# A linear-attention and channel-mix kernel with a written-out order: pairs in couples, one-piece q exponentials, single-DMA stores, a new order

## The chip, the cores and the metric

The kernel runs on one core of a Trainium2 chip. The metric is the device time of one launch in microseconds (us), the median over runs. Matrix products run on TensorE (PE), vector work on VectorE (DVE), exponentials and other activations on ScalarE (ACT), further elementwise work on GpSimd (POOL). SyncE (SP), POOL and ACT issue DMAs.

## The reference

There are 8 batches of 8 heads, 576 positions and 64 channels per head. Cut to what matters:

```
def phi(x):                                   # x: q or k
    proj = x @ w_phi                          # 64 -> 128 features
    proj = proj - max(abs(proj), axis=-1)
    return concat([exp(proj), exp(-proj)])    # 256 features
kv  = phi(k).T @ v ;  z = sum(phi(k))         # per head
att = (phi(q) @ kv) / (phi(q) @ z + 1e-6)     # 576 x 64 per head
x      = att, heads side by side              # 576 x 512 per batch
x_prev = x shifted by one position
xk = mu_k*x + (1-mu_k)*x_prev ;  xr likewise with mu_r
k  = relu(xk @ w_k)                           # 512 -> 1024
v  = (k*k) @ w_v                              # 1024 -> 512
out = sigmoid(xr @ w_r) * v
```

(As published, the reference subtracts the maximum before the minus sign is applied, so exp(-proj) carries the maximum with the opposite sign; the kernel does the same.)

## The kernel before

The heads are taken two at a time: pair n = 4b + a is pair a of batch b, 32 pairs in all. Each partition holds nine neighbouring positions of one head, 64 partitions a head. k and q of a pair lie side by side as nine blocks of 128 columns, two positions each; the middle block holds k's last position and q's first, and is handled as an "edge", for all four pairs of a batch at once (in three parts for batch 0). The second part works batch by batch on 8 blocks of 64 positions, in output tiles of 128 rows (`ci` 0 to 3); the ninth blocks of two batches form an edge tile, made once per two batches.

Everything is an operation with a name, given to `op()` and issued in the order of the text `ORDER`, written out in full. In it a word is a name, `:i` the PSUM buffer it writes, `/ENG` the engine that runs it, and `+n@i` says that n fill products on ones (L295) stand before it on PE. Every engine runs its own operations in that order. The names used here, with the pair number or batch.part behind them:

- `lk`, `lq`, `lv`: loads of k, q and v. `pt`, `pa`, `pb`: transposes on PE and copies for batches 0 and 1; later batches are transposed by DMA (`tr`).
- `kp`, `qp` (L561): projections, 8 products with 64 rows each. `rk`, `rq` (L574, L579): negated maxima of absolute values, 128x8, on DVE.
- `ea`, `eb` (L600): exponentials of k, plus and minus, 128x1024 on ACT. `em` (L586): exponentials of k's maxima, which `va`, `vb` (L592) multiply into v, mostly on POOL.
- `mh` (L610, L611): q's maxima split into two bf16 parts; `mt` (L615): their transpose on PE; `mc`: the copy out of PSUM; `qt` (L625, L631): q's projection with features on partitions, plus the maxima by products with the selector `sel`.
- `qa`, `qb` (L639): exponentials of q, each in two halves of 512. `kv` (L652, L658) and its copy `kc`; `nd` (L673): numerator and denominator; `ra`, `rd` (L681, L685): the division.
- `xz` (DMA transpose on SP) or `xt`, `xe`, `xf` (for the first 8 pairs, on PE): the result with channels on partitions; `xu`: the shifted copy; `df`, `xa`, `xb` (L722, L728): difference, xk and xr.
- `h`, `rl`, `sq`: product with w_k, relu, square, eight column blocks a batch; `r`, `th`: product with w_r, tanh; `v` (L836), `ob` (L842): product with w_v, output step; `so` (L849): two stores of 64 rows each. `he`, `rle`, `sqe`, `re`, `the`, `ve` (L920), `obe` (L924), `soe` (L929): the same for edge tiles.

`kp`, `qp`, `qt`, `kv` and the edge's `tp` and `qte` use products with 64 rows of the array, two side by side; all others use 128 rows. Large PSUM tiles have three buffers, one-bank tiles two. `h`, `r` and the edge products ask for all `xb` of the batch, and `xb` for `xa`.

Of the kernel before, what the change touches and what calls it, by code (L numbers as in the profile page):

```python
# [8 lines left out]
FP = mybir.dt.float32  # L9
# [10 lines left out]
ones hk hq ident dve2 hk.d hq.d wphi wphi.d lk0.1 lk0.1.d lq0.1 lq0.1.d lv0.0/SP lv0.0.d lk0.2  # L20
lk0.2.d dve3 mus mus.d lq0.2 lq0.2.d lv0.1/POOL lv0.1.d lk0.0.d/DVE lk1.0 lk1.0.d lv0.2/SP lv0.2.d
lq0.0.d/DVE pt0.0:0+9@0 lq1.0 lq1.0.d pt0.1:1 pa0/DVE pb0/ACT tr0 lk1.2 lk1.2.d dve1 tp0.0:0+1@2
kp0:1 rt0.0 qp0:2 lq1.2 lq1.2.d rk0 ekt0.0 pt1.0:1+1@0 eme0.0 pt1.1:0 wk.0 wk.0.d pa1/ACT pb1/DVE
tr1 mhe0.0/POOL rq0 ea0 kp1:0+2@2 eb0 rk1 qp1:2+2@0 mh0/POOL wk.1 wk.1.d wk.d mt0:1 em0 tp0.1:1
mte0.0:0 ea1 mce0.0/DVE va0/POOL mc0/DVE rt0.1 pt2.0:0 pt2.1:1 pa2/DVE ekt0.1 vb0/POOL pb2/DVE tr2
eb1 qt0:1 rq1 pt3.0:1 eme0.1 lv1.0/POOL lv1.0.d pt3.1:0 qa0 qp2:0 pa3/DVE kv0:2 mh1/POOL pb3/DVE tr3
rq2 wr.0 wr.0.d qte0.0:1 kc0/ACT em1 tp0.2:2 mhe0.1/POOL qb0 mt1:0 rt0.2 kp2:0 va1/POOL rk2 mc1/ACT
ekt0.2 qp3:1 eqe0.0 vb1/POOL kp3:2+1@0 rq3 ea2 mte0.1:0 mhe0.2/POOL pt4.0:1+2@1 eb2 mce0.1/DVE kv1:1
pa4/DVE mh2/POOL rk3 qte0.1:0 eme0.2 pt4.1:1 mh3/POOL nd0:0 eqe0.1 wr.1 wr.1.d wr.d em2 mt2:0
kc1/DVE mc2/ACT pb4/DVE tr4 wv.0 wv.0.d ea3 qt1:1 ra0 rd0 pt5.0:1 va2/POOL eb3 pt5.1:0 pa5/DVE qp4:0  # L30
pb5/DVE tr5 wv.1 wv.1.d wv.d mte0.2:1 qa1 rq4 qp5:2 pt6.0:0 vb2/POOL qb1 mce0.2/DVE pa6/DVE qte0.2:1
qt2:0 lk2.0 lk2.0.d rq5 em3 eqe0.2 xt0:0 va3/POOL kp4:1 qa2 xf0/DVE xe0/DVE kv2:2 rk4 mh4/POOL mt3:0
pt6.1:1 kc2/ACT df0/POOL qb2 nd1:2 mc3/DVE pb6/DVE tr6 mt4:0 ea4 ra1 nd2:0 mc4/DVE lq2.0 lq2.0.d rd1
pt7.0:0 eb4 lv1.2/POOL lv1.2.d ra2 xt1:1 rd2 kp5:2 vb3/POOL xf1/ACT xe1/ACT qt3:1 rk5 pa7/ACT
pt7.1:1 mh5/POOL kv3:0 qa3 xa0 xt2:0 xb0 qb3 pb7/DVE tr7 xf2/ACT df1/DVE xe2/ACT tp1.0:1 kc3/DVE ea5
rt1.0 df2/POOL nd3:0+1@1 eb5 ra3 mhe1.0/POOL rd3 ekt1.0 qt4:2+4@1 xa1 xt3:0 eme1.0 mt5:1 xb1 mc5/ACT
xe3/ACT qt5:1+1@2 xa2 qa4 mte1.0:1 qp6:0 xb2 xf3/ACT qb4 df3/DVE mce1.0/DVE xa3 em5 qte1.0:1+2@0 em4
kp6:2 xb3 eqe1.0 va4/POOL rq6 r0.0:0+3@0 qa5 h0.0:1 vb4/DVE qb5 rk6 mh6/POOL kv4:0 tr2.0 tr2.0.d tr8
tr9 rl0.0/ACT vb5/POOL qp7:1 th0.0 h0.1:1 rq7 ea6 va5/POOL r0.1:0 kc4/DVE em6 rl0.1/ACT sq0.0/DVE
tr2.2 tr2.2.d tr10 tr11 kv5:0 vb6/DVE th0.1 kp7:1 eb6 mh7/DVE mt6:1 h0.2:0 rk7 sq0.1/POOL nd4:2  # L40
lk3.0 lk3.0.d mc6/DVE em7 rl0.2/DVE h0.3:1 kc5/ACT lv2.0/SP lv2.0.d vb7/POOL ea7 ra4 rd4 lv2.2/SP
lv2.2.d h0.4:0 eb7 rl0.3/DVE va7/POOL qp8:2 xt4:1 rl0.4/ACT rq8 nd5:1 va6/POOL sq0.3/ACT qt6:0
sq0.2/ACT xf4/DVE xe4/DVE tp2.0:2 lq3.0 lq3.0.d ra5 qa6 h0.5:0 rd5 sq0.4/POOL qb6 rt2.0 h0.6:1 lk4.0
lk4.0.d rl0.5/ACT kv6:1 rl0.6/DVE df4/POOL ekt2.0 qp9:0 kc6/DVE h0.7:0 rq9 sq0.5/ACT mhe2.0/POOL
mt7:1 kp8:2 rl0.7/ACT kv7:1 mc7/DVE mh8/POOL rk8 sq0.7/ACT kp9:0 sq0.6/POOL mte2.0:0 r0.2:1 eme2.0
kc7/ACT em8 xa4 nd6:1 mce2.0/ACT th0.2 xb4 v0.0:0 ea8 rk9 vb8/POOL eb8 v0.1:1 va8/POOL em9 ob0.0 ea9
ra6 so0.0 so0.0.d rd6 mh9/POOL eb9 lq4.0 lq4.0.d qte2.0:0 ob0.1 qp10:1 vb9/POOL eqe2.0 qt7:2 rq10
qp11:0 tr3.0 tr3.0.d tr12 tr13 r0.3:1 qa7 va9/POOL rq11 xt5:0 th0.3 kp10:1 mh10/POOL qb7 xe5/DVE
xt6:1 xf5/DVE rk10 kv8:0 df5/POOL tr3.2 tr3.2.d tr14 tr15 xe6/ACT mt8:0 nd7:2 kc8/ACT xf6/DVE
mc8/DVE ea10 mt9:1 xa5 qt8:0 v0.2:0 eb10 df6/DVE mc9/DVE ra7 xa6 em10 qa8 xb5 qt9:1 xb6 qb8 v0.3:1  # L50
ob0.2 va10/POOL qa9 rd7 vb10/POOL mt10:0 nd8:0 qb9 mc10/DVE ob0.3 xt7:0 ra8 kv9:2 mh11/POOL xf7/ACT
rd8 xe7/ACT kv10:1 kc9/ACT df7/DVE xz8 xz8.d qt10:0 kc10/ACT xa7 kp11:2 qa10 nd9:1 xb7 mt11:0 qb10
rk11 r1.0:1 mc11/ACT nd10:0 ra9 th1.0 rd9 r1.1:0 em11 ea11 ra10 vb11/POOL xz9 xz9.d rd10 kp12:1
th1.1 h1.0:1 rk12 va11/POOL eb11 so0.1 so0.1.d qp12:0 h1.1:0 rq12 ea12 xu8/POOL xz10 xz10.d df8/POOL
qt11:2 rl1.1/ACT rl1.0/DVE tp3.0:0 eb12 lv3.0/SP lv3.0.d h1.2:0 rt3.0 sq1.0/POOL so0.2 so0.2.d qa11
kp13:1 rl1.2/DVE mh12/POOL h1.3:1 tr4.0 tr4.0.d tr16 tr17 qb11 sq1.1/DVE sq1.2/POOL h1.4:0 rl1.3/DVE
ekt3.0 xa8 r1.2:1 eme3.0 sq1.3/DVE rl1.4/ACT qp13:0 rk13 mhe3.0/POOL kv11:2 tr4.2 tr4.2.d tr18 tr19
th1.2 em12 xu10/POOL mt12:0 h1.5:1 sq1.4/ACT xu9/POOL mc12/DVE va12/POOL kc11/DVE ea13 rq13 h1.6:0
vb12/POOL rl1.5/ACT nd11:2 rl1.6/DVE lv3.2/SP lv3.2.d em13 sq1.5/ACT qp14:0 xb8 mte3.0:1 h1.7:0 eb13
mh13/POOL mce3.0/DVE ra11 he0.0:1 rd11 sq1.6/POOL rl1.7/ACT rq14 sq1.7/ACT xz11 xz11.d mt13:0 lk5.0  # L60
lk5.0.d kv12:2 rle0.0/ACT qt12:1 mc13/ACT df9/DVE kc12/ACT kp14:0 df10/DVE qa12 qte3.0:0 qt13:2 xa9
v1.0:1 eqe3.0 xa10 rk14 mh14/POOL qb12 vb13/POOL v1.1:0 ea14 xb9 eb14 va13/POOL ob1.0 nd12:1 ob1.1
em14 mt14:1 tp4.0:0 mc14/ACT ra12 qa13 vb14/POOL he0.1:0 rd12 rt4.0 qb13 xz12 xz12.d qp15:1
xu11/POOL va14/POOL r1.3:1 rle0.1/ACT rq15 lv4.0/SP lv4.0.d kp15:2 th1.3 df11/POOL re0:0 sqe0.0/ACT
rk15 ekt4.0 kv13:1 lq5.0 lq5.0.d v1.2:1 kc13/ACT xa11 ea15 xb11 eb15 xb10 kv14:1 em15 ob1.2 lk6.0
lk6.0.d qp16:0 kc14/ACT qt14:2 the0 rq16 qp17:1 mh15/POOL qa14 h2.0:1 sqe0.1/POOL rq17 nd13:0
rl2.0/ACT mhe4.0/POOL h2.1:0 qb14 ra13 mh16/POOL rd13 va15/POOL mt15:1 qp18:1 rl2.1/ACT kp16:2
mc15/DVE xz13 xz13.d rq18 qp19:0 sq2.0/ACT mte4.0:1 r2.0:0 sq2.1/POOL mce4.0/ACT eme4.0 rk16 so1.0
so1.0.d h2.2:1 th2.0 vb15/POOL h2.3:0 rq19 rl2.2/ACT so0.3 so0.3.d ea16 mt16:1 sq2.2/POOL nd14:1
mc16/DVE rl2.3/DVE so1.1 so1.1.d h2.4:1 eb16 xu12/POOL ra14 df12/DVE em16 kv15:0 rd14 rl2.4/ACT  # L70
va16/POOL qte4.0:0 kc15/ACT xz14 xz14.d qt15:2 eqe4.0 qt16:0 xu13/DVE kp17:1 sq2.3/DVE qa15 tr5.0
tr5.0.d tr20 tr21 h2.5:1 sq2.4/DVE vb16/POOL rk17 h2.6:0 rl2.5/ACT xa12 h2.7:1 rl2.6/ACT qb15
xu14/POOL v1.3:0 mh17/POOL tr5.2 tr5.2.d tr22 tr23 sq2.6/DVE ea17 rl2.7/DVE df13/DVE eb17 ve0:1
ob1.3 sq2.7/DVE em17 so1.2 so1.2.d xb12 qa16 mt17:0 mh18/DVE kv16:1 df14/POOL obe0 mc17/ACT so1.3
so1.3.d qb16 kp18:2 kc16/DVE r2.1:0 rk18 mh19/POOL mt18:1 nd15:0 sq2.5/POOL mc18/ACT th2.1 mt19:1
nd16:1 ra15 mc19/ACT ea18 rd15 vb17/POOL v2.0:1 ra16 xz15 xz15.d eb18 xa14 rd16 va17/POOL r2.2:0
soe0 soe0.d ob2.0 qt17:1 th2.2 xa13 lv4.2/SP lv4.2.d tp5.0:2 qa17 qt18:0 xz16 xz16.d xu15/POOL rt5.0
v2.1:0 qb17 xb14 lv5.0/SP lv5.0.d qa18 so2.0 so2.0.d mhe5.0/DVE v2.2:1 xb13 ekt5.0 ob2.1 df15/POOL
qb18 so2.1 so2.1.d mte5.0:0 kp19:2 ob2.2 kv17:1 rk19 mce5.0/ACT eme5.0 qp20:0 qte5.0:0 kc17/ACT em18
r2.3:1 eqe5.0 xa15 nd17:1 xb15 th2.3 v2.3:0 ea19 ra17 vb18/POOL rq20 eb19 va18/POOL rd17 kp20:0 em19  # L80
qp21:2 rk20 xz17 xz17.d lq6.0 lq6.0.d kv18:1 vb19/POOL h3.0:1 ob2.3 em20 kc18/ACT rq21 ea20 h3.1:0
mh20/POOL va19/POOL eb20 kp21:1 rl3.0/DVE qt19:2 rl3.1/DVE mh21/POOL r3.0:1 qa19 va20/POOL rk21
nd18:0 qb19 r3.1:0 vb20/POOL ra18 rd18 th3.0 kv19:2 em21 sq3.1/POOL xz18 xz18.d th3.1 qp22:0
kc19/ACT h3.2:1 rq22 ea21 vb21/POOL tr6.0 tr6.0.d tr24 tr25 mt20:0 nd19:2 eb21 mc20/DVE mh22/POOL
mt21:0 kv20:0 ra19 xu16/POOL rd19 sq3.0/ACT va21/POOL qt20:1 kc20/ACT rl3.2/DVE mc21/ACT kp22:2 qa20
qp23:0 df16/POOL rk22 tr6.2 tr6.2.d tr26 tr27 h3.3:0 qb20 h3.4:1 xu17/POOL rq23 xu18/POOL sq3.2/POOL
ea22 kv21:1 rl3.4/DVE lv5.2/POOL lv5.2.d eb22 nd20:0 so2.2 so2.2.d rl3.3/DVE h3.5:1 sq3.4/POOL ra20
sq3.3/ACT rd20 xz19 xz19.d mt22:0 kc21/ACT qt21:2 rl3.5/ACT mc22/DVE xa16 kp23:0 qa21 r3.2:0
lv6.0/SP lv6.0.d xb16 xz20 xz20.d h3.6:1 mh23/DVE th3.2 df17/DVE sq3.5/DVE h3.7:0 rl3.6/ACT so2.3
so2.3.d df18/DVE em22 sq3.6/DVE he1.0:1 rl3.7/ACT xa17 qb21 he1.1:0 sq3.7/DVE xb17 rle1.0/ACT  # L90
# [905 lines left out]
```

## Time and profile before

| what | value |
|---|---|
| three runs | 287.07 us median (286.09 to 287.44) |
| the profiled execution | 288.59 us, span 286.8 us |
| PE busy | 267.4 us, 93% of the span |
| DVE, ACT, POOL busy | 252.0, 227.1, 156.7 us |
| q exponentials (L639), 128 halves | 68.1 us |
| k exponentials (L600), 64 | 63.9 us |
| exponentials of k's maxima (L586), 64 | 11.4 us |
| stores, 72 of 128 KB | 2.4 us to landing (median) |

The span runs from the first to the last instruction of the profiled execution. Busy time of an engine is the union of its instructions; matmuls overlap, so a busy PE is not PE at its peak. Where operations follow closely, the time from one start to the next is less than the duration shown.

### The profile page before, as it was taken

Reading aid. Unit: us, or ns where it says so; the run is one execution under the profiler, and the core shown is the slowest. Engines: PE = TensorE matmul, PEld = TensorE weight load, DVE = VectorE, ACT = ScalarE, POOL = GpSimd, SP = SyncE. Lnnn points to the kernel's source line nnn. Section 1 sums busy time; section 2 is a strip of 40 time slices with the busy share of each in tenths; the row PEclk is TensorE's granted clock in tenths of the full one; section 3 lists DMA queues with packets and bytes.
Section 4 is the critical chain, followed back from the end, with each engine's and each line's share of the span. In section 5 each row is a group of like instructions: output and inputs, shape, how many; then the busy total and the mean of one; then the engine's idle time right before and its main releaser. Section 6 shows DMA issues by size and latency. Waiting matters only on the chain.

```text
span 286.8 us, 9054 instructions
## 1 busy us (share of the span) xinstructions
PE 267.4 (93%) x3729; PEld 154.4 (54%) x3729; DVE 252.0 (88%) x403; ACT 227.1 (79%) x488; POOL 156.7 (55%) x235
## 2 busy tenths in 40 slices
PE   6888889999999999999899989999999999999993
PEld 2556645556645656645556644565565646544541
DVE  6799999999999999999998999999999997873431
ACT  2699997999899899988879967799899979524710
POOL 8599637985567967644599446826356243300000
PEclk9799999999999999999999999999999999999998
DMA  7999989989768979995777959799831714345034
GB/s 170 219 240 248 208 196 221 193 140 197 107 86 208 209 126 199 172 209 125 230 109 103 225 160 162 173 136 187 145 49 41 197 39 98 28 94 126 22 74 110
DMA packets 65785, 42.89 MB, mean 150 GB/s; under 512 B 47120, under 2 KB 56720, under 8 KB 65744
## 3 DMA queue, kind: packets, MB, share of 16 engines
q1 hardware_dynamic: 54688, 28.19, 48.0%
q0 software_dynamic: 10912, 13.83, 27.8%
q8 instruction: 29, 0.48, 0.7%
q10 hardware_dynamic: 144, 0.29, 0.4%
q14 instruction: 12, 0.10, 0.1%
HBM read 33.62 MB, written 9.44 MB: 150 GB/s over the span
## 4 chain that ended last, share of the span: by engine, by line
PE 56%; DVE 21%; ACT 13%; DMA 4%; issue 4%; POOL 1%; SPq 0%; DVEq 0%; ACTq 0%
PE ps_h L803 16%; PE ps_v L836 12%; PE ps_r L822 8%; ACT k L600 5%; PE ps_kv L652 4%; DVE xr L728 4%; ACT q L639 4%; PE ps_nd L673 3%; DVE nmk L574 3%; DVE nmq L579 3%; DVE xk L728 3%; PE ps_q L561 2%; DMA wph_f<-in_w_phi_dram 2%; PE ps_k L561 2%; PE ps_qT L625 2%
## 5 line engine op out<-in xcount | busy, mean ns | idle before, releaser
L592 POOL TENSOR_TENSOR v<-vt,v 128x576 bf16<-128x576 f32 x57 | 72.4, 1284 | 42.9 <-ACT v L586 37.1
L639 ACT ACTIVATE q<-ps_qT 128x512 bf16<-128x512 f32 x128 | 68.1, 631 | 3.1 <-PE ps_qT L631 2.9
L600 ACT ACTIVATE k<-ps_k 128x1024 bf16<-128x1024 f32 x64 | 63.9, 1047 | 2.2 <-DVE nmk L574 1.9
L803 PE MATMUL ps_h<-xk,wk_bf 128*128 128x512 bf16 x256 | 61.6, 379 | 0.7 <-DVE mT L205 0.7
L836 PE MATMUL ps_v<-wv_bf,kk 128*128 128x512 bf16 x256 | 58.9, 379 | 0.0
L579 DVE TENSOR_REDUCE nmq<-ps_q 128x8 f32<-128x1024 f32 x32 | 38.7, 1214 | 1.9 <-PE ps_q L561 1.5
L836 PEld LDWEIGHTS <-kk 128*128 128x128 bf16 x256 | 24.2, 98 | 27.7
L574 DVE TENSOR_REDUCE nmk<-ps_k 128x8 f32<-128x1024 f32 x32 | 38.8, 1212 | 0.3 <-PE ps_k L561 0.2
L803 PEld LDWEIGHTS <-wk_bf 128*128 128x128 bf16 x256 | 22.9, 98 | 25.6 <-issue 1.3
L728 DVE SCALAR_TENSOR_TENSOR xr<-diff,mu_r_t,xs 128x576 bf16<-128x576 bf16 x32 | 33.8, 1065 | 0.0
L828 ACT ACTIVATE rt<-ps_r 128x512 bf16<-128x512 f32 x32 | 19.5, 609 | 17.6 <-PE ps_r L822 17.2
L209 ACT ACTIVATE krelu<-ps_h 128x512 bf16<-128x512 f32 x44 | 26.7, 606 | 7.6 <-PE ps_h L803 7.3
L822 PE MATMUL ps_r<-wr_bf,xr 128*128 128x512 bf16 x128 | 32.2, 379 | 0.2
L217 POOL TENSOR_TENSOR kk<-krelu 128x512 bf16<-128x512 bf16 x18 | 20.1, 1116 | 18.3 <-DVE krelu L211 11.1
L842 DVE SCALAR_TENSOR_TENSOR ob<-rt,ps_v 128x512 f32<-128x512 bf16 x32 | 21.5, 679 | 8.9 <-PE ps_v L836 7.5
L728 DVE SCALAR_TENSOR_TENSOR xk<-diff,mu_k_t,xs 128x576 bf16<-128x576 bf16 x32 | 28.1, 880 | 0.1
L685 DVE TENSOR_TENSOR x_sc<-ps_nd,rden 128x640 bf16<-128x640 f32 x32 | 26.2, 821 | 0.8
L722 POOL TENSOR_TENSOR diff<-xs 128x576 bf16<-128x576 bf16 x15 | 19.1, 1275 | 13.2 <-DVE mhl L610 4.1
L652 PEld LDWEIGHTS <-k 64*128 64x128 bf16 x1024 | 18.7, 94 | 7.0 <-issue 4.4
L561 PEld LDWEIGHTS <-qkT 64*128 64x128 bf16 x512 | 16.5, 95 | 11.0 <-issue 7.9
L652 PE MATMUL ps_kv<-v,k 64*128 64x65 bf16 x1024 | 21.9, 190 | 0.3 <-DVE x_sc L685 0.2
L673 PE MATMUL ps_nd<-kv,q 128*128 128x65 bf16 x512 | 21.4, 193 | 0.0
(102 smaller groups left out, 439.8 us busy)
## 6 DMA issues: line engine op xcount, KB each, us to landing
out_dram<-ob SPq DMA_DIRECT2D x72, 128.0 KB, 2.4
vt<-in_v_dram SPq DMA_DIRECT2D x12, 576.0 KB, 5.0
nat<-in_k_dram POOLq DMA_DIRECT2D x6, 576.0 KB, 8.5
nat<-in_q_dram POOLq DMA_DIRECT2D x6, 576.0 KB, 7.4
vt<-in_v_dram POOLq DMA_DIRECT2D x3, 576.0 KB, 11.5
wk_bf<-in_moe_w_k_dram POOLq DMA_DIRECT2D x2, 512.0 KB, 13.0
wv_bf<-in_moe_w_v_dram POOLq DMA_DIRECT2D x2, 512.0 KB, 10.1
nat<-in_k_dram POOLq DMA_DIRECT2D x3, 288.0 KB, 9.2
```

What stands on the lines that cost most here:

```text
L561: nc.tensor.matmul(ps[:, par, g * 128:(g + 1) * 128], lhsT=qkT[b][r, g0 + gg + g, :], rhs=wph[r, :], start=(g == 0), stop=(g == 3))
L574: nc.vector.tensor_reduce(s["nmk"], s["k"].rearrange("p a (g f) -> p (a g) f", f=128), axis=AX.X, op=ALU.max, apply_absolute_value=True, n ...
L579: nc.vector.tensor_reduce(s["nmq"], s["q"].rearrange("p a (g f) -> p (a g) f", f=128), axis=AX.X, op=ALU.max, apply_absolute_value=True, n ...
L592: (nc.vector if eng == "DVE" else nc.gpsimd).tensor_tensor(vb[:, a, pn, :, 0:64], vt[b, a // 2][:, a % 2, :].rearrange("p (s d) -> p s d", ...
L600: nc.scalar.activation(s[f"k{pn}"], s["k"].rearrange("p a (g f) -> p (a g) f", f=128), AF.Exp, scale=(1.0 if pn == 0 else -1.0))
L639: nc.scalar.activation(t[:, h, :].rearrange("f (g a p) -> f g a p", g=4, a=2), s["qT"].rearrange("f a (g h p) -> f h g a p", g=4, h=2)[:, ...
L652: nc.tensor.matmul(ps[:, hh, pn * 65:(pn + 1) * 65], lhsT=s[f"k{pn}"][r, c, :], rhs=vb[r, a, pn, 2 * g + par, :], start=(pn == 0 and c == ...
L673: nc.tensor.matmul(ps[:, bk, o * 65:(o + 1) * 65], lhsT=tail if sl < 2 else s[f"q{pn}"][:, h, G * 128:(G + 1) * 128], rhs=s["kv"][:, h, pn ...
L728: nc.vector.scalar_tensor_tensor(out=t[:, a, (b % 2) * S:(b % 2 + 1) * S], in0=s["d"], scalar=mu[:, a:a + 1], in1=xs[:, a, 0:S], op0=ALU.m ...
L803: nc.tensor.matmul(ps, lhsT=wk_bf[:, c, fc * 128:(fc + 1) * 128], rhs=xkt[bp][:, c, m0:m0 + 512], start=(c == 0), stop=(c == NDC - 1))
L822: nc.tensor.matmul(ps, lhsT=xrt[bp][:, c, m0 + ci * 128:m0 + (ci + 1) * 128], rhs=wr_bf[:, c, :], start=(c == 0), stop=(c == NDC - 1))
L836: nc.tensor.matmul(ps, lhsT=s["kk"][:, fc, ci * 128:(ci + 1) * 128], rhs=wv_bf[:, fc, :], start=(fc == 0), stop=(fc == NFC - 1))
```

## The change

Pairs 0 to 3 stay alone (`ONE = 4`); from pair 4 on, pairs 2i and 2i+1 form a couple. Their `rq` and `rk` write into one tile each, and one `mh`, `mt`, `mc` and `em`, named after the first pair, serve both. Each `qa` and `qb` is one instruction over 1024 columns, and `nd` reads its weights from the new layout. A `so` is one DMA of 128 rows. `xb` no longer asks for `xa`; `h` and `he` ask for the `xa`, `r` and `re` for the `xb`. The last edge tile's `ve`, `obe` and `soe` are made in two column halves of 256, with a store for each batch and half, one of the four issued by ACT. `ORDER` is another one throughout, with other engines for many operations, 36 fill products instead of 29.

```
+        w = 1 if n < ONE else 2
+        u, c0 = (n, a) if w == 1 else (n - n % 2, a - a % 2)
+        first, last = n == u, n == u + w - 1
+        cp = cpl.setdefault(u, {})
...
         def em():
             for pn in range(2):
-                nc.scalar.activation(vb[:, a, pn, 0:8, 64].rearrange("p (g r) -> p r g", r=2),
-                                     s["nmk"].rearrange("p (r g) -> p r g", r=2), AF.Exp,
+                nc.scalar.activation(vb[:, c0:c0 + w, pn, 0:8, 64].rearrange("p a (g r) -> p a r g", r=2),
+                                     cp["nmk"][:, 0:w, :].rearrange("p a (r g) -> p a r g", r=2), AF.Exp,
                                      scale=(1.0 if pn == 0 else -1.0))
...
-            nmv = s["nmq"].rearrange("p (a g) -> p a g", a=2)
-            e.tensor_copy(mhv[:, 1, 0], nmv)
-            e.tensor_tensor(mhv[:, 1, 1], nmv, mhv[:, 1, 0], op=ALU.subtract)
+            nmv = cp["nmq"][:, 0:w, :].rearrange("p k (a g) -> p k a g", a=2)
+            e.tensor_copy(mhv[:, 0:w, 0], nmv)
+            e.tensor_tensor(mhv[:, 0:w, 1], nmv, mhv[:, 0:w, 0], op=ALU.subtract)
...
-                    nc.tensor.matmul(ps[:, par, g * 128:(g + 1) * 128], lhsT=sel[r, 4 + g, :],
-                                     rhs=s["mT"][r, :], start=False, stop=(g == 3))
+                    nc.tensor.matmul(ps[:, par, g * 128:(g + 1) * 128], lhsT=sel[r, 4 * j + g, :],
+                                     rhs=cp["mT"][r, :], start=False, stop=(g == 3))
...
-                for h in range(2):
-                    nc.scalar.activation(
-                        t[:, h, :].rearrange("f (g a p) -> f g a p", g=4, a=2),
-                        s["qT"].rearrange("f a (g h p) -> f h g a p", g=4, h=2)[:, h],
-                        AF.Exp, scale=(1.0 if pn == 0 else -1.0))
+                nc.scalar.activation(
+                    t.rearrange("f x (a p) -> f x a p", a=2),
+                    s["qT"].rearrange("f a (x p) -> f x a p", p=64),
+                    AF.Exp, scale=(1.0 if pn == 0 else -1.0))
...
-                for i in range(2):
-                    nc.sync.dma_start(out=main[2 * ci + i], in_=s["o", ci][64 * i:64 * i + 64, :])
+                nc.sync.dma_start(out=main[2 * ci:2 * ci + 2], in_=s["o", ci])
...
+        for hf in range(1 if bp < 3 else 2):
+            w = DM if bp < 3 else DM // 2
...
+            for i in ((-1,) if bp < 3 else (0, 1)):
+                x = "so" + nmv + ("" if i < 0 else ".a" if i == 0 else ".b")
+                e = "ACT" if hf == 1 and i == 1 else "SP"
```

The start of the two orders, around the loads of batch 1:

```
-lq0.0.d/DVE pt0.0:0+9@0 lq1.0 lq1.0.d pt0.1:1 pa0/DVE pb0/ACT tr0 lk1.2 lk1.2.d dve1 tp0.0:0+1@2
+lv0.2.d pt0.1:1 pa0/DVE pb0/ACT tr0 dve1 tp0.0:0+1@2 kp0:1 rt0.0 qp0:2 rk0 eme0.0 mhe0.0/POOL ekt0.0
+pt1.0:1+1@0 lk1.0 lk1.0.d pa1/ACT mte0.0:0 rq0 ea0 lq1.0 lq1.0.d pt1.1:1+2@2 pb1/DVE tr1 lk1.2
```

## The prediction

> **What bounds the kernel now.** I read the busy shares first, then the same shares stage by stage, then PE's own timeline, the chain of waits at the start, and the tail.
>
> ```profile
> PE 267.4 (93%) x3729; PEld 154.4 (54%) x3729; DVE 252.0 (88%) x403; ACT 227.1 (79%) x488; POOL 156.7 (55%) x235
> ```
>
> ```profile
> 0.00:43.50 43.50, 35.35 (x560) 22.49 (x561) 39.09 (x81) 35.04 (x86) 31.29 (x57) 0.96 1.08 213
> 43.50:82.00 38.50, 36.96 (x656) 22.51 (x654) 37.88 (x60) 35.31 (x77) 27.19 (x33) 1.00 0.87 158
> 82.00:184.00 102.00, 97.46 (x1417) 56.48 (x1417) 98.94 (x139) 88.17 (x191) 68.95 (x105) 1.00 0.88 174
> 184.00:263.00 79.00, 78.53 (x994) 43.52 (x991) 68.86 (x112) 60.33 (x124) 29.27 (x43) 1.00 0.54 98
> ```
>
> Columns of the second: stretch, length, busy PE, PEld, DVE, ACT, POOL, PE clock, DMA share, GB/s. Three engines look almost full until 184 us, so busy time does not say which one binds. PE's timeline does:
>
> ```profile
> 38.62 0.39 PE L631 MATMUL ps_qT<-mT,sel 64*128 64x128 bf16 x8
> 38.94 0.23 PE L488 MATMUL ps_me<-ident,mhlt 128*128 128x128 bf16 x1
> 39.10 0.40 PE L561 MATMUL ps_q<-wph,qkT 64*128 64x128 bf16 x8
> ...
> 43.35 1.03 PE L803 MATMUL ps_h<-xk,wk_bf 128*128 128x512 bf16 x4
> 44.31 0.42 PE L652 MATMUL ps_kv<-v,k 64*128 64x65 bf16 x16
> ...
> 44.87 0.38 PE L561 MATMUL ps_q<-wph,qkT 64*128 64x128 bf16 x8
> 45.19 1.04 PE L803 MATMUL ps_h<-xk,wk_bf 128*128 128x512 bf16 x4
> ```
>
> Start to start, an undisturbed `h` (four products) takes 0.863 us, but 0.96 when a 64-row product follows (43.35 to 44.31); `qp` takes 0.223 alone and 0.32 when a 128-row product follows (44.87 to 45.19). So each change between 64-row and 128-row products costs PE 0.096 us either way, and "busy" hides it. With the list of ORDER laid beside the timeline, every operation gets its undisturbed step: `h`, `r`, `re` 0.863 (100 of them), `v`, `ve` 1.727 (36), `he` 0.89 (8), `kp`, `qp` 0.223 (64), `qt` 0.44, `kv` 0.563, `nd` 0.636, `mt` 0.056 (32 each), the rest 11.8: 235.9 us of work. ORDER has 142 changes of row mode: 13.6 us. The last product ends at 282.15, so PE waited or ran fill products for 32.6 us: 21.0 before the first MoE product (`r0.0`, 42.5 us), 11.6 after it, mostly in 34 places, none over 1.2 us. After 42.5 us PE binds at 95%; before it something else does:
>
> ```profile
> 24.58 1.96 ACT q L639 x4
> ...
> 29.59 1.83 ACT k L600 x2
> ...
> 40.08 0.11 ACT xs L203
> ...
> 42.49 1.02 PE ps_r L822 x4
> ```
>
> These lines of the chain of waits (start, length) show the start running along ACT's exponentials to `xf3` at 40.1, then over DVE's `df3`, `xa3`, `xb3` (ended 42.3) to `r0.0`. DVE is 98% busy from 10 to 40 us as well.
>
> ```profile
> 280.25 1.89 PE L920 MATMUL ps_ve<-wv_bf,kke 128*128 128x512 bf16 x8
> 282.24 0.69 DVE L924 SCALAR_TENSOR_TENSOR ob<-rt,ps_ve 128x512 f32<-128x512 bf16 x1 [1.04 <-PE ps_ve L920]
> 282.95 1.10 SPq L929 DMA_DIRECT2D out_dram<-ob  x2
> ```
>
> The tail: product, output step, two issues in a row on SP, then landing and end at 286.8.
>
> **The change, part by part.** The sum is made in the profiled span (286.8; that execution took 288.59, so 1.8 lies around it, and it stands 1.5 above the median 287.07). The difference is taken off the median.
>
> *Couples.* From pair 4 on, 28 `mh`, `mt`, `mc` and `em` become 14. PE: 14 x 0.056 = 0.8 us of work, 0.7 of it after the first MoE product. POOL: 14 x 0.415 (0.27 and 0.145 start to start) = 5.8, off the path, since POOL is busy 55%. ACT: a small exponential takes 0.098, so 28 x 0.098 = 2.7 less; the joined one has 16 elements a row instead of 8, so between 0.098 and 0.196 each (gain 0 to 2.7; I take 2.5, as its length counts little). ACT and DVE `mc`: 14 x 0.13 to 0.16 = 2.
>
> *q exponentials in one piece.* Two halves step 0.477 each, the k exponential of equal size 0.904: 64 x 0.05 = 3.2 us of ACT. The access alternates between two banks in runs of 64, as the halves did; bounds per exponential 0.904 (a k) and 0.954 (no gain). I take the k's. In the start, ten of them stand before `xe3`: 0.5 us. The Trainium skill, "ScalarE: Activation LUTs", section on the cost of ACT_TABLE_LOAD, gives an ACTIVATE 186 ns of fixed cost, of which about 93 overlap with the one before; by that, a joint would save 93 ns, as an estimate 6.0 us in all. The steps above say 50 ns, and they are used. After 42.5 us none of this shortens PE's list.
>
> *New order.* Engines change too: `sq` on ACT 19 to 24, `xu` on ACT 4 to 12, `rl` on ACT 44 to 48, `kc` on DVE 7 to 13. With start-to-start steps, the whole queues change by: DVE 228.3 to 225.5, ACT 211.5 to 209.2, POOL 147.5 to 140.1, PE work 235.9 to 235.1. Row-mode changes fall from 142 to 132: 1.0 us. Fill products grow from 29 to 36, 35 of them before `h0.0`, where PE waits anyway; uncovered the seven cost 1.5.
>
> *Start.* `h` now needs only the `xa`, and `h0.0` comes before `xb2` and `xb3` are needed. ACT's queue through the last copy that `df3` needs is 28.8 us in the old list and 29.5 in the new; 0.55 of it is the cast of q, which falls into ACT's wait before 6.3 us: 28.95. So that copy ends at 40.3 instead of 40.2; `xf3`, `df3`, `xa3` add 0.1 + 0.37 + 0.73 and handovers 0.2: `h0.0` at 41.7. By DVE's queue (31.85 through `xa3` against 32.9 through `xb3`, counted from the first copy) it is 41.3. I take 41.7: 0.8 gained, bounds 0 and 1.2. On POOL's queue the batch-1 loads now stand behind `mhe0.0`, which waits for DVE until 8.6: issue at about 9.0 instead of 4.7, landing by about 4.3 later (15.7 and 20.1 become 20.0 and 24.4 at worst) for transposes that ran at 20.05 and 24.96. Just covered; if not, 0 to 1.5 us.
>
> *From the first MoE product to the last.* PE's list there: old work 218.4 and 100 changes (9.6), sum 228.0; new 217.6 and 96 (9.2), sum 226.8: 1.2 gained. The waits: 11.6 now, of which 1.6 stand before `mt` and 1.1 before `qt`. Half of the `mt` are gone; I take half of their 1.6, 0.7 to 0.8, and leave the other waits alone. Bounds: all 11.6 gone, or 6 more.
>
> *Stores.* 32 pairs of issues (0.47 and 0.59) become 32 single ones of twice the size: 17 us off SP, between 0.47 and 1.06 each. SP mostly waits, so nothing.
>
> *Tail.* The last edge tile is made in two halves of 256 columns. The first half's output step and stores hide under the second half's 0.86 us of products. Then half an output step (0.69 becomes about 0.39; 0.3 to 0.69) and one issue instead of two in a row, as the other goes by ACT: SP is free 1.07 after its first issue. Old: last issue 1.31 after the last product; new: about 0.7. Gain 0.6, bounds 0 and 0.8. The Trainium skill, "DMA: Bandwidth & Descriptors", Rules for kernel authors, says that spreading DMAs over issuing engines only saves issue time, not transfer time. If the split of issues gave nothing, the tail would gain the 0.3 of the output step alone.
>
> Sum: 0.8 + 1.2 + 0.7 + 0.6 = 3.3 us. 287.07 - 3.3 = 283.8.
>
> **Rivals.**
>
> *Slower: the first pair of a couple starves `kv`.* `em` now waits for both `rk`; one `rk` steps 1.13 us.
>
> ```profile
> POOL v L592 <- ACT v L586: 37.1, 13, 5.4
> ```
>
> POOL already waits 37.1 us for `em`, so a later `em` moves the `v` products one for one, and `kv` needs both. In ORDER, PE's work between `em` and `kv` shrinks from 7.8 to 5.5 us (median; smallest 2.7 to 2.1), while `em` and two products need 0.2 + 2 x 1.15 = 2.5. Behind a waiting `kv` stands all of PE. Full price 14 x 1.13 = 15.8; it outweighs the 3.3 gained from 0.24 us a couple on. At 0.4 a couple: 5.6 lost, 2.3 net, 289.4. Against it: waits before `kv` are now 0.4 us in all.
>
> *No change.* PE's shorter list only meets DVE and ACT earlier, which are 97% and 86% busy from 82 to 184 us; the 1.2 and 0.7 turn into waits and the loads eat the start: 0.6 left, 286.5.
>
> *More.* The list is new throughout; if half of the 11.6 us of waits goes (5.8 instead of 0.7), the gain is 8.4: 278.7; a third gone (3.9) gives 280.6.
>
> **How the numbers follow.** Forecast (282.3 to 285.6) 0.58, more 0.12, no change 0.18, slower rival 0.12. What a measurement here can tell from no change is about 0.5%, 1.4 us. Faster 0.70, same 0.18, slower 0.12. The range leaves out the far part of "more" and the slower rival beyond 1.3 us: 280.0 to 288.4.
>
> **What would show it.** Right: `h0.0` near 41.7; 18 `mt`; PE's last product near 279.5 with waits after the first MoE product near 11; the span's end 4.0 after the last product; q at about 1.05 us for 1024. Wrong: new waits of PE before `kv` ended by `v` products; transposes of batch 1 waiting for loads; waits after 42 us above 14 us or below 7.

## The result, and the profile after

The changed kernel takes 343.94 us (median of four runs, 342.6 to 346.74) where the kernel before takes 287.25: a ratio of 1.200, 95% interval 1.190 to 1.210. 283.8 was forecast. The profiled execution took 346.74 us, its span is 345.0. (Ratios here compare only runs within 1.5% of the fastest of their kernel; medians are over all runs.)

The same views as before, of the changed kernel. First the busy times and what the DMA queues carried (packets, MB, time of the packets as a share of 16 engines' span):

```profile
PE 272.7 (79%) x3682; PEld 159.7 (46%) x3730; DVE 236.7 (69%) x388; ACT 223.8 (65%) x413; POOL 141.1 (41%) x193
...
q1 hardware_dynamic: 53536, 27.54, 65.0%
```

The kernel before had, in the last of these lines:

```profile
q1 hardware_dynamic: 54688, 28.19, 48.0%
```

PE's busy time hardly grew (272.7 against 267.4 us), but its share of the span fell from 93 to 79%. DVE, ACT and POOL have less work, as planned, and are idle longer. Only SP's queue q1 has a larger share: 65.0% of a longer span, where it had 48.0%, for 2% fewer bytes. The stretches (same columns as in the prediction; the DMA share adds up the times of packets, so it can exceed 1 where packets overlap):

```profile
0.00:43.50 43.50, 38.13 (x618) 24.40 (x623) 39.22 (x80) 37.47 (x80) 32.33 (x54) 1.00 1.08 216
43.50:82.00 38.50, 30.64 (x537) 19.51 (x545) 30.04 (x49) 29.75 (x54) 24.96 (x28) 0.91 1.27 157
82.00:184.00 102.00, 81.97 (x1185) 48.06 (x1202) 75.56 (x112) 72.12 (x130) 46.40 (x64) 0.92 0.93 128
184.00:263.00 79.00, 65.59 (x915) 38.54 (x923) 56.61 (x90) 55.27 (x98) 25.95 (x38) 0.91 1.07 116
...
327.00:345.00 18.00, 0.00 (x0) 0.00 (x0) 0.75 (x2) 0.00 (x0) 0.00 (x0) 0.61 0.19 60
```

Until 43.5 us all is well: PE has done more than before (38.13 against 35.35 us). Then PE, DVE, ACT and POOL lose busy time together, while the DMA engines are busier than before (1.27 against 0.87 in the second stretch) and move no more (157 against 158 GB/s). PE's clock is lower too (0.91 to 0.92, before 1.00), but that is a small part of the loss: PE is busy 6.7 us longer than in `split_stores` below (266.0 us). An engine that all others wait for is not among the four. The chain of waits names it (start, length; the longest pieces from three of its windows):

```profile
64.12 13.65 DMA qkT<-nat
...
106.93 24.38 DMA xs<-x_sc
...
192.52 21.18 DMA out_dram<-ob
...
224.28 11.28 DMA xs<-x_sc
```

Transposes (`tr`, `xz`), and output tiles that wait for a free buffer, are on the chain for 11 to 24 us each; before, no DMA piece of the chain behind the first load (5.6 us) was longer than 3.9 us. The first of the four is the weakest sign: it begins before the first main store is issued (71.10 us), and 9.43 us of it are there with the stores split as well. SP's own timeline shows them stuck at the issue:

```profile
106.93 13.40 SPq L700 DMA_TRANSPOSE xs<-x_sc  x1
120.42 0.54 SPq L855 DMA_DIRECT2D out_dram<-ob  x1
121.01 6.21 SPq L700 DMA_TRANSPOSE xs<-x_sc  x1
```

One issue of `xz` takes 13.40 us; with the stores split (below) it is mostly 1.2 to 1.3. The cause can be read where nothing but stores runs, here after PE's last product (326.55) and in the tail:

```profile
326.00:330.00 4.00, 0.55 (x6) 0.25 (x3) 0.75 (x2) 0.00 (x0) 0.00 (x0) 1.00 0.13 51
338.00:342.00 4.00, 0.00 (x0) 0.00 (x0) 0.00 (x0) 0.00 (x0) 0.00 (x0) 0.50 0.13 51
```

The last two numbers are the mean busy share of the 16 DMA engines and GB/s: 0.13 of 16 is two engines, moving 51 GB/s. A store of 256 KB therefore takes 5.1 us (262144 / 51000), and 32 of them keep these two engines for 164 us, as an estimate. Before, each store of 128 KB landed in 2.4 us (median). The Trainium skill, "DMA: Bandwidth & Descriptors", section "Why a DMA increments its semaphore by 16 and not by 1", states the rule: a DMA runs on the largest number of engines up to 16 that divides the slowest dimension (other than 1) of both access patterns. `main[2 * ci:2 * ci + 2]` is 2 x 64 x 512, so two; 64 rows of 512 gave 16. The trace agrees with it.

The tail, last of all:

```profile
324.74 4.94 SPq L855 DMA_DIRECT2D out_dram<-ob  x1
324.75 1.80 PE L928 MATMUL ps_ve<-wv_bf,kke 128*128 128x256 bf16 x15
...
328.06 0.75 DVE L934 SCALAR_TENSOR_TENSOR ob<-rt,ps_ve 128x256 f32<-128x256 bf16 x2 [3.47 <-DMA out_dram<-ob]
...
329.78 6.54 SPq L941 DMA_DIRECT2D out_dram<-ob  x3
```

The last output steps wait for older stores, and the span ends 18.45 us after the last product (before: 4.66), while the backlog drains.

### The profile page after: what moved, and what is told of

It reads as the page before. It is cut to its first block, busy times and chain, and to the rows that moved or that the text cites. A ratio compares the mean times of both kernels' runs of the same rounds, so it can differ in the third digit from the quotient of the medians.

```text
span 345.0 us, 8816 instructions
## 1 busy us (share of the span) xinstructions
PE 272.7 (79%) x3682; PEld 159.7 (46%) x3730; DVE 236.7 (69%) x388; ACT 223.8 (65%) x413; POOL 141.1 (41%) x193
## 3 DMA queue, kind: packets, MB, share of 16 engines
q0 software_dynamic: 11056, 14.42, 24.7%
## 4 chain that ended last, share of the span: by engine, by line
PE 40%; DMA 30%; DVE 11%; issue 5%; POOL 4%; SPq 3%; ACT 3%; DVEq 0%; ACTq 0%; POOLq 0%
DMA xs<-x_sc 17%; PE ps_h L810 12%; DMA out_dram<-ob 9%; PE ps_v L843 7%; PE ps_r L829 5%; DMA qkT<-nat 4%; PE ps_kv L656 3%; POOL v L597 3%; PE ps_nd L677 2%; SPq L700 2%; DVE nmq L584 2%; PE ps_q L566 2%; DVE x_sc L689 2%; PE ps_k L566 2%; PE ps_qT L630 1%
## 5 line engine op out<-in xcount | busy, mean ns | idle before, releaser
L597 POOL TENSOR_TENSOR v<-vt,v 128x576 bf16<-128x576 f32 x59 | 68.6, 1184 | 38.6 <-ACT v L591 28.0
L643 ACT ACTIVATE q<-ps_qT 128x1024 bf16<-128x1024 f32 x64 | 63.6, 1046 | 2.4 <-PE ps_qT L636 2.3
L726 POOL TENSOR_TENSOR diff<-xs 128x576 bf16<-128x576 bf16 x15 | 20.2, 1346 | 62.9 <-ACT xs L706 32.1
L206 ACT ACTIVATE krelu<-ps_h 128x512 bf16<-128x512 f32 x48 | 28.8, 606 | 11.6 <-PE ps_h L810 11.6
L214 POOL TENSOR_TENSOR kk<-krelu 128x512 bf16<-128x512 bf16 x18 | 19.1, 1068 | 30.6 <-ACT krelu L206 24.9
L656 PEld LDWEIGHTS <-k 64*128 64x128 bf16 x1024 | 20.3, 96 | 16.4 <-issue 13.1
L656 PE MATMUL ps_kv<-v,k 64*128 64x65 bf16 x1024 | 23.7, 194 | 4.4 <-issue 3.9
L732 DVE SCALAR_TENSOR_TENSOR xk<-diff,mu_k_t,xs 128x576 bf16<-128x576 bf16 x32 | 26.4, 830 | 0.3 <-POOL diff L726 0.2
L732 DVE SCALAR_TENSOR_TENSOR xr<-diff,mu_r_t,xs 128x576 bf16<-128x576 bf16 x32 | 26.5, 832 | 0.1
L566 PEld LDWEIGHTS <-qkT 64*128 64x128 bf16 x512 | 17.6, 98 | 11.7 <-issue 8.2
```

The costliest lines, as they stand in the source:

```text
L566: nc.tensor.matmul(ps[:, par, g * 128:(g + 1) * 128], lhsT=qkT[b][r, g0 + gg + g, :], rhs=wph[r, :], start=(g == 0), stop=(g == 3))
L597: (nc.vector if eng == "DVE" else nc.gpsimd).tensor_tensor(vb[:, a, pn, :, 0:64], vt[b, a // 2][:, a % 2, :].rearrange("p (s d) -> p s d", ...
L643: nc.scalar.activation(t.rearrange("f x (a p) -> f x a p", a=2), s["qT"].rearrange("f a (x p) -> f x a p", p=64), AF.Exp, scale=(1.0 if pn ...
L656: nc.tensor.matmul(ps[:, hh, pn * 65:(pn + 1) * 65], lhsT=s[f"k{pn}"][r, c, :], rhs=vb[r, a, pn, 2 * g + par, :], start=(pn == 0 and c == ...
L732: nc.vector.scalar_tensor_tensor(out=t[:, a, (b % 2) * S:(b % 2 + 1) * S], in0=s["d"], scalar=mu[:, a:a + 1], in1=xs[:, a, 0:S], op0=ALU.m ...
```

## The experiments

Theory A: the merged store runs on two engines, and what needs these two waits. Rivals: B, couples, new order or 1024-column exponentials make the waits; C, 256 KB at once is too much, whatever the number of engines.

**The stores split again, all else changed** (`split_stores`, and a second time as `split_again`):

```
-                nc.sync.dma_start(out=main[2 * ci:2 * ci + 2], in_=s["o", ci])
+                for i in range(2):
+                    nc.sync.dma_start(out=main[2 * ci + i], in_=s["o", ci][64 * i:64 * i + 64, :])
```

> The changed kernel, with only the 32 main stores written again as two DMAs of 64 rows (128 KB) each; couples, one-piece q exponentials, new order and split tail stay. Theory A (the merged store runs on two of the 16 DMA engines, and all that SP queues behind it on those two waits): the stores land in about 2.4 us again, the pieces of 'DMA xs<-x_sc' of 24 and 21 us vanish from the chain, and the time falls to 283.8 (280 to 286.5), what the prediction's other steps give. Theory B (couples, new order or the 1024-column exponentials make the waits, and the store's form is innocent): 335 or more. Theory C (the size of a store or its number is what counts): also below 290, as the size is halved; the run with 256 KB stores of another pattern tells A and C apart.

Measured: 282.56 us (278.32 to 286.53, six runs) against 287.46; ratio 0.975 (0.970 to 0.980). The second time:

> The split-store run once more, unchanged, so that the run with the earlier loads is compared with it on the same chip: 282.5 (280 to 285), as before.

Measured: 284.38 (279.32 to 288.84) against 287.61; ratio 0.974 (0.968 to 0.980). The other parts of the change gain 2.5%; the stores' form costs 61 us between the medians (343.94 less 282.56), 64 between the lowest runs (342.60 less 278.32). B is out. In the second stretch PE, DVE, ACT and POOL are busier than with merged stores, and the DMA engines move more (175 against 157 GB/s) at a smaller share (1.03 against 1.27):

```profile
43.50:82.00 38.50, 35.56 (x620) 21.98 (x613) 33.89 (x56) 34.91 (x60) 26.41 (x30) 0.96 1.03 175
```

The page's chain of `split_stores`:

```profile
PE 80%; DVE 7%; DMA 5%; POOL 3%; ACT 2%; issue 1%; SPq 0%; DVEq 0%; POOLq 0%
```

**The merge alone, in the kernel before** (`before_merged`, the reverse edit):

> The kernel before, with only its 32 pairs of main stores merged into 32 DMAs of 256 KB (outermost step of two); old order, no couples. Theory A: slower by tens of us, 330 to 350, stores landing in 5 us or more, the granted DMA share 0.13 where only stores run. Theory B: 287, as nothing of the new order is in it.

Measured: 355.3 us (354.35 to 358.43), ratio 1.238 (1.233 to 1.243), a little more than expected. The merge alone is enough. Where only its stores run, from 334 to 338 us, the DMA share is 0.13 at 51 GB/s, as expected. Its chain has DMA pieces of the same kind, in the window from 60 to 240 us:

```profile
127.72 13.66 DMA xs<-x_sc
...
180.44 14.13 DMA qkT<-nat
200.19 19.41 DMA xs<-x_sc
```

**The same bytes in one DMA, with 8 or 4 outermost.** Which 128 of a batch's 512 tokens form a tile is free, as long as `r` and `v` take the same ones:

```
-        lhsT=s["kk"][:, fc, ci * 128:(ci + 1) * 128]
+        lhsT=s["kk"][:, fc, ci:512:4]                     # and xrt likewise
-        nc.sync.dma_start(out=main[2 * ci:2 * ci + 2], in_=s["o", ci])
+        nc.sync.dma_start(out=main[:, ci::4], in_=s["o", ci])
```

With 4 it is `ci // 2 * 256 + ci % 2` in steps of 2, and `main[ci // 2 * 4:ci // 2 * 4 + 4, ci % 2::2]`.

> The changed kernel with one DMA of 256 KB to a main store as it has, but each tile of 128 rows taken as every fourth token of the 512 rather than 128 neighbours (the weight loads of the v and r products read with a step of four), so that the store's outermost step is 8 instead of 2; bytes, rows of 2 KB and number of DMAs are the same. Theory A: eight engines instead of two, a store lands in about a quarter of the 5.1 us plus what is fixed, some 2 us, and the time is 284 to 290. Theory C (256 KB at once is too much): 335 or more, as in the changed kernel.

> As the run with the outermost step of 8, but with every second token of 256, so that the outermost step is 4. Theory A: four engines, 2.5 to 3 us for a store, time between the run with 8 and the changed kernel: 286 to 305. Theory C: 335 or more.

Measured: 284.04 us with 8 (277.78 to 289.12) and 307.8 with 4 (295.57 to 312.16, a wide spread; the median is just over what was expected, the lowest run within it), beside 343.94 with 2. C is out: size, rows and number of DMAs are the same in all three. In the records of single packets, counting the store's packets of 2 KB that are in flight at one time, 2 is the commonest number of the changed kernel (for 148 us), 4 with four outermost (75 us), 8 with eight (30 us); before, it is 16.

**Whose ring?** Everything on SP stands in one queue with the stores. Does the order in it do the harm, or are the two engines full?

```
-                nc.sync.dma_start(out=main[2 * ci:2 * ci + 2], in_=s["o", ci])
+                nc.scalar.dma_start(out=main[2 * ci:2 * ci + 2], in_=s["o", ci])
```

> The changed kernel with its 32 merged stores as they are (256 KB, outermost step 2), but issued from ScalarE's queue instead of SyncE's. It tells two forms of theory A apart. A1 (order in one ring: what SP issues behind a store on the two engines waits for it, while the engines themselves have room): the transposes that SP issues no longer stand behind stores, the long 'DMA xs<-x_sc' pieces go, and the time is what the split stores on ScalarE give, plus at most the longer landing of the last stores: 285 to 300. A2 (the two engines are simply full, whichever queue feeds them): transposes, which use all 16 engines, still wait for the two, and the time stays above 320. Store issues cost ScalarE 32 x about 0.5 us in both.

> The control of the run before: stores of 128 KB in pairs, as in the split run, but issued from ScalarE's queue. Both forms of theory A: 283 to 292, as ScalarE pays 64 issues of about 0.5 us (32 us, beside some 55 us in which it is idle) and waits for the output steps of VectorE ahead of its exponentials.

Measured: merged on ScalarE 351.14 (338.88 to 355.15), split on ScalarE 302.32 (296.8 to 305.09). The merge costs 49 us there between the medians and 42 between the lowest runs, on SP 61 and 64; both on ScalarE are rough, as three of the four merged runs lie 11 to 16 us above the lowest. Transposes that SP issues with no merged store in its queue still wait, in the chain of `merged_on_act`:

```profile
73.75 14.51 DMA xs<-x_sc
128.49 18.77 DMA qkT<-nat
```

The control has no such `xs<-x_sc`, but a long transpose of batch 3, `64.91 16.95 DMA qkT<-nat`, that began before any main store; so a long `qkT<-nat` alone is no sign of merged stores. By the times, the two engines being full is the larger part (A2), and the order in SP's ring can be at most the rest. The control missed its range by 10 us: PE waits 10.8 us for that one transpose, where it waits 2.5 in `split_stores` (9.2 in `merged_on_act`), and 4.5 us for a relu of ScalarE. So this is no clean price of the ring.

**Eight stores at a time.**

```
+                if b in (1, 2):        # early8;  late8: b >= 6
+                    nc.sync.dma_start(out=main[2 * ci:2 * ci + 2], in_=s["o", ci])
+                    return
```

> The split-store run with only the 8 main stores of batches 1 and 2 merged again (256 KB, outermost step 2); the other 24 stay in pairs. They are issued between about 100 and 145 us, where SP also brings transposes and loads. Theory A (two full engines): the transposes behind them land late, PE waits there; the tail stays as in the split run (4.2 us from the last product to the span's end). A store keeps two engines for 5.1 us, 41 us in all within a stretch of some 45 us, so 5 to 25 us are lost: 288 to 307. If only stores queued without pause over the whole kernel do harm (a backlog of all 32), nothing much: 281 to 285.

> The split-store run with only the 8 main stores of the last two batches merged again. Behind them SP issues no load and, after about 250 us, no transpose. Theory A: PE's last product comes as in the split run (274.6 in its profile, within 3), and only the tail grows, because the last four or five stores come every 2 to 3 us and leave every 5.1: the span ends 10 to 16 us after the last product instead of 4.2, 290 to 298 in all. If merging hurts by a cost for each DMA rather than by engines, the tail stays near 5: 283 to 285.

Measured: early 309.08 (306.21 to 312.8; ratio 1.070, 1.063 to 1.077), late 297.47 (293.21 to 303.97; ratio 1.028, 1.021 to 1.036). `early8`: a tail of 3.8 us, and 24.7 us more than `split_again`; the median is slightly over the bound. Its chain has, among others:

```profile
136.21 18.12 DMA vt<-in_v_dram
...
178.14 21.80 DMA out_dram<-ob
```

`late8`: the last product at 276.79, as in the split run, and a tail of 18.5 us (10 to 16 expected), with the same signature, and an output step waiting for a store's buffer:

```profile
274.00:280.00 6.00, 2.79 (x21) 1.76 (x18) 1.44 (x3) 0.60 (x1) 0.00 (x0) 1.00 0.13 51
```

```profile
266.95 11.28 DMA out_dram<-ob
```

So a merged store costs a wait where transposes and loads share the engines, and a backlog in the tail. In whole: the changed kernel's last product is 52.0 us behind that of `split_stores` (326.55, 274.56), its tail 14.2 longer; the sum is the 66.2 between the spans, 345.0 and 278.8.

**The one-piece q exponentials**, alone in the kernel before, and taken out of the split run:

```
-                t = s[f"q{pn}"] = mid.tile([128, 2, 512], BF, ...)
-                for h in range(2):
-                    nc.scalar.activation(t[:, h, :]..., s["qT"]...[:, h], AF.Exp, ...)
+                t = s[f"q{pn}"] = mid.tile([128, 8, 128], BF, ...)
+                nc.scalar.activation(t..., s["qT"]..., AF.Exp, ...)
```

> The kernel before, with only the q exponentials in one piece of 1024 columns instead of two of 512; stores in pairs, old order. If PE's list binds after the first MoE product, as the prediction has it, 3.2 us of ScalarE bring only what they shorten in the start: 0.5 us, 286.5 to 287. If ScalarE's exponentials still hold PE's products up in the middle, 1 to 3 us: 284.5 to 286.

> The split-store run with the q exponentials in two halves again. If the new order and the couples carry the gain over the kernel before: 282.5 to 283.5, as before less 0.5 or so. If the joined exponentials carry it: 285 or more. A step of two halves should take 0.95 us against 0.90 to 0.92 for the joined one.

Measured: in the old order 289.55 against 287.74, ratio 1.006 (1.003 to 1.008): slightly slower. In the new order halves give 281.71 (278.39 to 288.69), ratio 0.971 (0.967 to 0.975), which the joined form's 0.975 (0.970 to 0.980) can't be told from. ACT's busy time does fall, 227.1 to 223.8, and the first `h` comes 0.7 us earlier in the old order (42.7); afterwards PE waits 13.6 us instead of 11.6 (283.35 - 41.72 - 228.0: end of the last product, start of the first MoE product, PE's list between them). Why an earlier ACT ends in more waits there stays open. The gain over the kernel before is that of the new order, the couples and the split tail; these weren't taken apart.

**Earlier loads.** In `split_stores` one long DMA piece is left on the chain behind the first load, `64.12 9.43 DMA qkT<-nat`: batch 3's second transpose, and PE waits for it:

```profile
PE ps_e L466 <- DMA qkT<-nat: 2.5, 1, 2.5
```

In `ORDER`, `lk3.0` and `lq3.0` move up POOL's queue to directly behind `va6`:

```
-... va6/POOL h0.4:0 ... qa7 lk3.0 lk3.0.d tp2.0:0 ... eme2.0 lq3.0 lq3.0.d rk8 ...
+... va6/POOL lk3.0 lk3.0.d lq3.0 lq3.0.d h0.4:0 ... qa7 tp2.0:0 ... eme2.0 rk8 ...
```

> The split-store run with the two loads of batch 3 (k and q) moved ahead on POOL's queue by two squares, one split and one v product, to directly behind the v product of pair 6: about 1.3 and 3.7 us earlier. In the split run the second transpose of that batch stands on the chain for 9.4 us (64.1 to 73.6), and PE waits 2.7 us for it. If that wait is set by when the loads end, as the chain says, the transposes go 3 us earlier and 2 to 3 us are gained on the split run: 279.5 to 281. If the transposes only meet the next loads instead, no change: 282 to 283.

Measured: 276.40 us (275.69 to 277.46), ratio 0.961 (0.957 to 0.965), the best version; by the ratios 3.8 us are gained on `split_again`, more than expected. The transpose is off the chain, and batch 1's first `h` stands at 77.2 us instead of 81.9 (83.0 in `split_again`). The wait costs more than its own 2.5 to 3.0 us: from 72 to 80 us, behind it, PE's granted clock is 0.79 in both split runs and 1.00 here, which is 1.7 us. With the wait gone the six runs lie within 1.8 us; those of the two split runs spread over 8 and 10. That the late transpose makes that spread is likely: `late8` has the same early stores, and in its profile PE waits 5.5 us for this transpose, with a clock of 0.72 from 72 to 84 us (0.86 in `split_stores`). What makes it later in one run than in another stays open.

```profile
PE 83%; DVE 11%; POOL 3%; issue 1%; ACT 0%; POOLq 0%
```

## Why the prediction was wrong

The step that failed is the one on stores: "32 pairs of issues (0.47 and 0.59) become 32 single ones of twice the size: 17 us off SP ... SP mostly waits, so nothing." It counted the issues and left out the transfer. The term was 0; measured, it is 61 us, because the transfer ran on two DMA engines and transposes waited for them. The diff had what was needed: the size of the outermost dimension went from 64 to 2. And the prediction's own table shows that a longer transfer would not be free: DMA engines 0.87 to 0.88 busy from 43.5 to 184 us, with transposes that PE needs in the same queue. None of the rivals was this one; the slower rival, `kv` starved by the first pair of a couple, has the sign but not the mechanism. POOL's wait for `em` is no longer than before (37.1 us then) in `split_stores`, and no `v` product holds up a `kv`:

```profile
POOL v L597 <- ACT v L591: 30.1, 11, 7.6
```

The other steps can be read in `split_stores`, which is the change without its stores. That its medians, 282.56 and 284.38, stand on both sides of the 283.8 is chance: the runs behind them spread over 8 and 10 us, and the terms of the sum are not met. In the profiled executions (288.59 and 280.56 us):

| term | predicted gain | measured |
|---|---|---|
| first MoE product | 0.8 | 2.35 (42.5 to 40.15) |
| PE's list after it | 1.2 | 1.2, taken from the list, not measured |
| waits of PE after it | 0.7 | 4.0 (11.6 to 7.6) |
| tail | 0.6 | 0.4 (4.66 to 4.24) |
| sum | 3.3 | 8.0 |

- Start: ACT's last whole copy for `df3` was put at 40.3. It begins at 37.89 and takes 0.73, so the sum over ACT's queue was 1.7 too long, as it kept waits that the new list does not have; the chain now runs over DVE (`xk`, `xr`, `nmq`) instead. In the changed kernel itself `h0.0` stands at 39.69:

```profile
39.35 0.40 PE L636 MATMUL ps_qT<-mT,sel 64*128 64x128 bf16 x8
39.69 1.04 PE L810 MATMUL ps_h<-xk,wk_bf 128*128 128x512 bf16 x4
```

- Waits (274.56 - 40.15 - 226.8 = 7.6): the waits before `mt` are gone altogether, not by half, and most of the others too; from 82 to 263 us PE shows no idle time in `split_stores`. That is the rival "more", a third of the waits gone. Of the 7.6, 2.5 are one transpose and 1.7 the lower clock behind it, and with `earlier_loads` these go as well.
- q: 1.05 us for 1024 columns, as forecast, and 3.3 us off ACT; worth nothing that shows at the end, where the step gave 0.5 us in the start, and slightly negative in the old order.
- Loads of batch 1: issued from 8.66 us, landed from 15.4 to 19.9 in `split_stores`; covered, as forecast.

## What to carry to other kernels

Before two DMAs are made one, write out both access patterns and look at the outermost dimension: fewer issues are worth less than fewer engines cost, here 17 us of an idle sequencer against 61 us of the kernel. When all compute engines go idle together and a DMA queue's share grows without more bytes, look for a stretch where one kind of transfer runs alone and turn its DMA share into engines (0.13 x 16 = 2). After a reordering, follow the last DMA piece left on the chain back to its loads; moving two of them up was worth more here (3.8 us) than all the work saved on ACT.

## What the runs showed of the hardware

- One DMA engine moved about 25 GB/s of 2 KB rows (51 GB/s on two).
- A transfer confined to two engines holds up transposes issued by another engine's queue too: the merge cost 49 us between the medians on ScalarE's queue, 61 on SP's.
- Weights read in steps of two elements loaded as fast as neighbouring ones (98 ns, median); in steps of four a load took 113 ns (161.3 us in all against 155.0). The products took 379 ns (median) in all three, so none of it shows in PE's products.
- Behind a wait of PE the granted clock was mostly lower: 0.79 from 72 to 80 us behind waits of 2.5 and 3.0 us, 0.72 from 72 to 84 us behind waits of 4.2 (`one_dma_outer8`) and 5.5 us (`late8`); in `split_q_halves` a wait of 2.5 us left it at 1.00.
